# Two layers of FNet mixing and a spatial-shift MLP: normed rows kept on chip, z3 blocks ahead of w3 weights, operand work dealt over w4 steps

## The chip, the cores and the metric

The kernel runs on one core of a Trainium2 chip. The engines of a core run their own instruction lists side by side: PE (TensorE, the matrix engine), DVE (VectorE), ACT (ScalarE), POOL (GpSimd) and SP (SyncE), which here issues all transfers, one after the other in the order of the program. The metric is the device time of one execution in microseconds (us).

## The reference

The input x has 2048 rows (tokens) of 512 values. A layer adds a Fourier mixing and a shift MLP, and the whole is run twice with the same weights:

```python
def _A_ref(x, Cr, Ci, Dr, Di):              # FNet mixing
    a = x @ Dr.T ; b = x @ Di.T
    return Cr @ a - Ci @ b

def _B_ref(x, w1, w2, w3, w4):              # spatial-shift token mixing, channel MLP
    h  = gelu(layernorm(x) @ w1)
    g  = h with its four column quarters shifted by +1, -1, +2, -2 rows (zeros come in)
    x1 = x + g @ w2
    return x1 + gelu(layernorm(x1) @ w3) @ w4

for layer in range(2):
    x = x + _A_ref(layernorm(x), ...)
    x = x + _B_ref(layernorm(x), ...)
```

Cr and Ci are 2048 x 2048, Dr and Di 512 x 512, w1 and w2 512 x 512, w3 512 x 1376, w4 1376 x 512, all fp32.

## The kernel before

**Numbers.** Every fp32 operand is used as two fp32r parts: a high part, cast by ScalarE, and a low part, which VectorE makes as the operand minus its high part. A product takes three matmuls, high x high, high x low and low x high (`mm3`, L275 to L278).

**Fourier mixing.** The DFT matrices come in pieces of 512 KB from `in_ws` and `in_hs` into four buffers `raw`. `stage_one` (L207) makes the high part, or a difference and its high part, in one of four slots `ring`; `stage_two` (L233) makes the low part. `issue_dma` (L194) loads the next piece when a buffer is free, up to `state["load"]`; `state["limit"]` says up to which item operands are made ahead. The other operand is the normed rows. For each of the eight tiles of two row blocks, `xs[k]`, there are statistics (`xp_stats`), normed rows (`xp_norm`), sums and differences of their halves (`ax_sums`, `ay_sums`), their high parts and their low parts (`ax_highs`, `ay_highs`, `ax_lows`, `ay_lows`). The table `BACK` (L38) says after which step of a later phase rows of x1 are read back into `xs`.

**Shift MLP.** `by_pairs` (L753) treats the rows in four chunks of 512. For each chunk `shifted` does the w1 product and the gelu into `rg` (L653 to L659) and `mixed` the w2 product. Tables of functions, filled by `D(slot)` for VectorE and `A(slot)` for ScalarE (L900 to L990), say which operand work is done beside which step. `u_stats`, `finish` and `turn3` norm a chunk's rows and turn them; the turned rows z3 go to HBM (`z3d`) and are read back as blocks `b11f`, `b21f`, `b12f`, `b22f` (`b_in`, L738).

The w3 and w4 products are made for two pairs of chunks, one after the other. In a pair, five steps p make the w3 products of two blocks of the hidden width f each by seven products b1, b6, b5, b2, b7, b4, b3 of half blocks and of their sums, `bt1` to `bt4` (instead of eight), whose operands are parts of the w3 weights and of the z3 blocks. The results pass through the gelu into `hc` and are split into `h`. One chunk's w4 product follows in the steps beside them, and after the last p come the rest of its steps and thirteen steps of the other chunk, of 12 matmuls each (`w4_part`, L1003). Each w4 step uses one load of 512 KB (`w4_load`, L842); there are six slots, four in layer 0's second pair. `drain` (L1011) adds the accumulators to `xs` when a chunk's w4 product is done, and frees their banks.

In layer 0 the weights w3 and w4 are split once and written to HBM (`w3d`, `w4d`), and afterwards only read; `w3b` has two buffers of 1792 KB.

**What sets the order around the change.** All orders are written by hand, in program order. The list `bg` is emptied one function at a time by `one()` (L1021) in the p steps; `early` joins it in the last pair of layer 0, and `then[k]` (L1044) holds what `after_part(k)` (L1165) does behind w4 step k. These two lists make the next layer's first rows while this layer ends.

Of the kernel before, what the change touches and what calls it, by code (L numbers as in the profile page):

```python
# [8 lines left out]
F32 = mybir.dt.float32  # L9
# [28 lines left out]
BACK = {1: (0,), 2: (2,), 4: (4,)}  # L38
# [4 lines left out]
def spectral_mlp_kernel(ctx: ExitStack, tc: tile.TileContext, x, ws, hs, w1, w2, w34, out):  # L43
# [351 lines left out]


    mr_of = {}

    def ax_norm(k):
        mr_of[k] = xp[k]  # L400
        xp_norm(k)
# [351 lines left out]
    def by_pairs(layer, zs, xin, dst):  # L753
# [222 lines left out]
        if layer == 0:  # L976
# [8 lines left out]
            A(30, lambda: w4_high(0), lambda: w4_high(1))  # L985
            D(31, lambda: w4_low(0))
# [39 lines left out]
        early, then = [], [[] for _ in range(NF + 2)]  # L1026
        if not last_of(layer):

            def more():
                state.update(limit=w_items[1], load=len(pieces))  # L1030
                issue_dma()

            def do(f, k):
                return lambda: f(k)

            for k in range(4):
                early += [do(f, k) for f in (xp_stats, ax_norm, ax_sums, ax_highs, ax_lows)]
            early += [do(f, k) for f in (ay_back, ay_norm) for k in (0, 1)]
            for i, f, k in (
                *((0, ay_sums, 0), (0, ay_highs, 0), (0, ay_sums, 1), (0, ay_highs, 1)),  # L1040
                *((1, ay_lows, 0), (1, ay_back, 2), (2, ay_lows, 1), (2, ay_back, 3)),
                *((3, xp_stats, 4), (3, ay_norm, 2), (4, ay_sums, 2), (4, ay_highs, 2)),
                *((5, ay_lows, 2), (5, ay_norm, 3), (6, ay_sums, 3), (6, ay_highs, 3), (6, xp_norm, 4)),
                *((7, ay_lows, 3), (7, ax_sums, 4), (7, ax_highs, 4), (8, ay_sums, 4), (8, ax_lows, 4)),  # L1044
                *((8, ay_highs, 4), (9, xp_stats, 5), (10, ay_lows, 4), (10, xp_norm, 5)),
                *((11, ax_sums, 5), (11, ax_highs, 5), (12, ax_lows, 5)),
            ):
                then[i].append(do(f, k))
            then[1].insert(0, more)
            for i in (9, 11, 12):  # L1050
                then[i].append(lambda: ahead(1))

        for pair in range(n_pairs):
            c1, c2 = 2 * pair, 2 * pair + 1
            kept, next_too = layer or pair, pair == n_pairs - 1 and not last_of(layer)
            hcs = [hc[:, f] for f in range(NF)]
            if next_too:
                hcs[8:] = [hx[:, 0], hx[:, 1], rest[0]]
                bg += early
            bk, acc1 = (acc4, mm4) if pair == 0 else (mm4, acc4)  # L1060
            acc2 = [bk[(1 + i) % 4] for i in range(4)]
            if pair == 0:
                bg += [] if layer else [u_stats(2, 2)]
                bg += [finish(2, 0), finish(2, 2), turn3(turned, 2, 0, 1), turn3(turned, 2, 2, 3)]
                bg += [lambda: turn_out(turned, z3d[2])]
                z3_last = lambda t: [
                    *(u_stats(3, 0), u_stats(3, 2), finish(3, 0), finish(3, 2)),
                    *(turn3(t, 3, 0, 1), lambda: (turn3(t, 3, 2, 3)(), turn_out(t, z3d[3]))),
                ]
                bg += z3_last(turned if layer else tmp[:, 0:4])  # L1070
# [16 lines left out]
            def split_later(k):  # L1087
                if k < NF:
                    split(h4[(2 + k) % 4], hcs[fs[k]], act)

# [16 lines left out]
            for p in range(NF // 2):  # L1107
# [15 lines left out]
                add(u, u, b2)  # L1123
                low1 = gelu_high(h4[2 * (p % 2)], u)
# [7 lines left out]
                low1()  # L1132
                at_point(3)
# [17 lines left out]
                if kept or p + 2 >= NF // 2:  # L1151
                    w3_load(NF // 2 * pair + p + 2)
                one()

            if pair == 0:
                for c, names in ((2, ("11", "21")), (3, ("12", "22"))):
                    for half, to in enumerate(names):
                        b_in(c, half, to)
                bg += [sum_of("t1", "12", "11"), sum_of("t2", "22", "t1"), sum_of("t3", "22", "12"), sum_of("t4", "21", "t2")]
                bg += [parts(b) for b in ("11", "21", "12", "22", "t2", "t1", "t3", "t4")]  # L1160
# [4 lines left out]
            def after_part(k):  # L1165
                if next_too:
                    for f in then[k]:
                        f()
# [6 lines left out]
            for j in range(c1 * TC, c1 * TC + TC, 2):  # L1175
# [230 lines left out]
```

## Time and profile before

| | before |
|---|---|
| median of 3 runs (lowest to highest) | 1478.5 us (1477.55 to 1480.68) |
| profiled execution, its own time | 1479.15 us |
| its span in the trace | 1477.2 us |
| mean granted clock of TensorE | 0.994 |
| PE busy | 1452.9 us (98%), 6344 matmuls |
| DVE / ACT / POOL busy | 1121.6 / 721.9 / 80.5 us |
| moved by transfers | 288.97 MB, 196 GB/s mean |

Busy times are those of one profiled execution; its span is 1.95 us shorter than its time, which also holds what lies around the first and the last instruction. Times of events below are counted from the start of the span. A matmul counts as busy while it waits in the pipeline, so a busy share of 98% does not by itself say that TensorE ran at its pace; the count of matmuls in a window of 20 us says it.

### The profile page before, as it was taken

The page shows a single profiled execution, that of the slowest core. Times are in us where ns is not written, and L with a number is a line of the kernel's source. Part 1 is how long each engine was busy: PE and PEld are TensorE (multiplying, and loading weights), DVE is VectorE, ACT ScalarE, POOL GpSimd, SP SyncE. Part 2 cuts the span into 40 slices and gives each one's busy share as a digit, 9 for nine tenths or more (in the row PEclk, how much of TensorE's full clock was granted, in tenths as well). Part 3 has the DMA queues.
Part 4 walks back from the last instruction along what each step waited for, and adds up shares of the span by engine and source line. Part 5 has one row for each costly group of instructions (what it writes and reads, how often), then busy time and mean ns, then how long its engine had stood idle before and what let it go on. Part 6 is the DMA issues. An engine that isn't in the chain of part 4 may idle for free.

```text
span 1477.2 us, 17273 instructions
## 1 busy us (share of the span) xinstructions
PE 1452.9 (98%) x6344; PEld 1189.0 (80%) x6344; DVE 1121.6 (76%) x1553; ACT 721.9 (49%) x966; POOL 80.5 (5%) x111
## 2 busy tenths in 40 slices
PE   9999999999999999899889999999999999999998
PEld 7888888888878787688767888888888788888887
DVE  6876987988868897566589879979888688646443
ACT  5563454444567655344545544544445675333231
POOL 2100000000001000000010000000000010000000
PEclk9999999999999999999999999999999999999999
DMA  6326556566546678845635465565565457758434
GB/s 238 133 87 212 191 189 212 179 199 236 179 136 178 214 254 280 327 151 185 243 113 173 169 199 200 185 202 194 185 236 184 141 165 274 224 213 300 158 131 157
DMA packets 111876, 288.97 MB, mean 196 GB/s; under 512 B 8496, under 2 KB 37168, under 8 KB 109232
## 3 DMA queue, kind: packets, MB, share of 16 engines
q1 hardware_dynamic: 111792, 287.87, 57.8%
q8 instruction: 50, 0.82, 0.2%
q14 instruction: 34, 0.28, 0.1%
HBM read 243.01 MB, written 44.83 MB: 195 GB/s over the span
## 4 chain that ended last, share of the span: by engine, by line
PE 83%; DVE 9%; DMA 4%; ACT 2%; issue 1%; POOL 1%; SPq 0%; DVEq 0%; ACTq 0%; POOLq 0%
PE psd L276 9%; PE psd L277 9%; PE psd L278 9%; PE psa L276 7%; PE psa L278 7%; PE psa L277 7%; PE psc L278 6%; PE psc L276 6%; PE psc L277 6%; PE psb L278 6%; PE psb L276 6%; PE psb L277 6%; DMA w4r<-w4d 2%; DVE ring L239 2%; DMA raw<-in_ws 1%
## 5 line engine op out<-in xcount | busy, mean ns | idle before, releaser
L223 ACT CAST ring<-raw 128x1024 fp32r<-128x1024 f32 x127 | 132.8, 1054 | 100.1 <-PE psd L278 48.9
L239 DVE TENSOR_TENSOR ring<-raw,ring 128x1024 fp32r<-128x1024 f32 x127 | 154.6, 1221 | 26.8 <-ACT ring L223 26.8
L276 PE MATMUL psd<-ring,rr 128*128 128x512 f32 x208 | 80.9, 389 | 0.0
L277 PE MATMUL psd<-ring,rr 128*128 128x512 f32 x208 | 80.9, 389 | 0.0
L278 PE MATMUL psd<-ring,rr 128*128 128x512 f32 x208 | 80.9, 389 | 0.0
L653 ACT ACTIVATE tmp<-rest 128x512 f32<-128x512 f32 x32 | 20.3, 633 | 82.4 <-DVE rest L473 82.1
L316 POOL TENSOR_TENSOR rs<-ve,mhalf 128x4 f32<-128x4 f32 x16 | 26.8, 1678 | 612.8 <-DVE nm L315 612.8
L656 DVE TENSOR_TENSOR h<-hc,h 128x512 fp32r<-128x512 f32 x41 | 27.9, 689 | 38.3 <-ACT h L659 38.2
L659 ACT CAST h<-hc 128x512 fp32r<-128x512 f32 x41 | 25.5, 621 | 64.4 <-PE psc L277 26.9
L230 ACT CAST ring<-ring0f 128x1024 fp32r<-128x1024 f32 x28 | 29.6, 1056 | 54.3 <-DVE ring0f L229 54.3
L324 ACT ACTIVATE tmp<-xs,nb,rs 128x512 f32<-128x512 f32 x58 | 44.8, 810 | 23.1 <-POOL nb L296 23.1
L239 DVE TENSOR_TENSOR ring<-ring1f,ring 128x512 fp32r<-128x512 f32 (+1 forms) x56 | 53.3, 952 | 0.8 <-ACT ring L226 0.8
L295 POOL TENSOR_TENSOR rs<-ve,mhalf 128x2 f32<-128x2 f32 (+1 forms) x33 | 30.2, 914 | 429.8 <-DVE nb L294 429.8
L276 PE MATMUL psc<-ring,ay 128*128 128x512 f32 x128 | 49.9, 390 | 0.3 <-ACT rr11f L498 0.3
L277 PE MATMUL psc<-ring,ay 128*128 128x512 f32 x128 | 50.0, 391 | 0.2 <-DVE ring L239 0.2
L278 PE MATMUL psc<-ring,ay 128*128 128x512 f32 x128 | 49.8, 389 | 0.0
L276 PE MATMUL psb<-ring,ay 128*128 128x512 f32 x128 | 49.8, 389 | 0.0
L277 PE MATMUL psb<-ring,ay 128*128 128x512 f32 x128 | 49.8, 389 | 0.0
L278 PE MATMUL psb<-ring,ay 128*128 128x512 f32 x128 | 49.8, 389 | 0.0
L276 PE MATMUL psd<-ring,ay 128*128 128x512 f32 x126 | 49.0, 389 | 0.0
L276 PE MATMUL psa<-ring,ay 128*128 128x512 f32 x126 | 49.0, 389 | 0.0
L277 PE MATMUL psd<-ring,ay 128*128 128x512 f32 x126 | 49.0, 389 | 0.0
(450 smaller groups left out, 4451.6 us busy)
## 6 DMA issues: line engine op xcount, KB each, us to landing
raw<-in_ws SPq DMA_DIRECT2D x183, 512.0 KB, 4.9
w4r<-w4d SPq DMA_DIRECT2D x77, 512.0 KB, 3.7
raw<-in_hs SPq DMA_DIRECT2D x56, 512.0 KB, 3.5
w3b<-w3d SPq DMA_DIRECT2D x15, 1792.0 KB, 7.3
w3d<-w3b SPq DMA_DIRECT2D x5, 1792.0 KB, 6.7
x1d<-tmp SPq DMA_DIRECT2D x12, 512.0 KB, 6.3
xs<-x1d SPq DMA_DIRECT2D x12, 512.0 KB, 6.7
w4d<-w4r SPq DMA_DIRECT2D x11, 512.0 KB, 7.4
```

The source lines that it names most:

```text
L223: nc.scalar.copy(dest[:, a:b, 0], r[0][:, a:b])
L230: nc.scalar.copy(dest[:, :, 0], lo)
L239: nc.vector.tensor_tensor(lo, src, hi.bitcast(F32), op=ALU.subtract)
L276: nc.tensor.matmul(o, lh, rh, start=first, stop=False)
L277: nc.tensor.matmul(o, lh, rl, start=False, stop=False)
L278: nc.tensor.matmul(o, ll, rh, start=False, stop=last)
L295: nc.gpsimd.tensor_tensor(rs[:, :n], ve[:, :n], mhalf[:, 0, :n], op=ALU.pow)
L316: nc.gpsimd.tensor_tensor(rs, ve, mhalf[:, :, :2], op=ALU.pow)
L324: nc.scalar.activation(o, s, AF.Identity, bias=mr[2], scale=mr[1])
L653: nc.scalar.activation(g_of, ps_of, AF.Gelu_apprx_tanh)
L656: nc.vector.tensor_tensor(dst[:, 1], g, dst[:, 0].bitcast(F32), op=ALU.subtract)
L659: copy(dst[:, 0], g)
```

## The change

- `norm_in_place` norms tiles 2 and 3 of the next layer's rows into `xs` itself, so that the sums made later read them there. Before, such tiles were written to `x2d` and read back through `tmp` (`ay_back`) and normed again (`ay_norm`).
- The reads of the second pair's z3 blocks are placed in the last p step of the first pair, ahead of further w4 loads; the two w3 loads move behind them into the w4 steps.
- The raw loads, row writes, sums and parts between and after the pairs are dealt over the w4 steps by `then` for both pairs; before, raw loads were issued in one go and the row work lay in other steps.
- In the table beside `shifted`, the parts of the blocks and of their sums are in another order, and the parts of t3 and t4 move into the pair loop. `u_stats(3, 2)` moves behind `finish(2, 2)`.
- At the start, the low part of item 1 is made in two halves, the first tile is normed in halves, up to four items are made ahead instead of two, and the low parts of tile 1 come ahead of a low part of the ring.
- One read back of x1 rows moves from step 4 to step 6.

The core of the diff:

```diff
-BACK = {1: (0,), 2: (2,), 4: (4,)}
+BACK = {1: (0,), 2: (2,), 6: (4,)}
...
-        nc.vector.tensor_tensor(lo, src, hi.bitcast(F32), op=ALU.subtract)
+        for i in ((1, 0) if n == 1 else (slice(0, b - a),)):
+            nc.vector.tensor_tensor(lo[:, i], src[:, i], hi[:, i].bitcast(F32), op=ALU.subtract)
...
-    def ay_back(k):
-        xp[k] = pairs[k % 2]
-        rows(xp[k], x2d, 2 * k, 2, True)
-
-    def ay_norm(k):
+    def norm_in_place(k):
         for i in range(2):
-            normed_act(xp[k][:, i], xp[k][:, i], mr_of[k][i])
+            normed_act(xs[k][:, i], xs[k][:, i], xp[k][i])
+        xp[k] = xs[k]
...
-        A(26, highs("12"))
-        D(27, sum_of("t2", "22", "t1"), sum_of("t4", "t4", "t2"))
-        A(27, highs("22"))
-        D(28, lows("12", "22"))
-        A(28, highs("t2", "t1"))
-        D(29, lows("t2", "t1"))
+        A(27, highs("12", "22"))
+        D(28, sum_of("t2", "22", "t1"), sum_of("t4", "t4", "t2"))
+        A(28, highs("t1", "t2"))
+        D(29, lows("12", "22"))
         A(29, highs("t3", "t4"))
-        D(30, lows("t3"))
-        D(31, lows("t4"))
+        D(31, lows("t2", "t1"))
...
-            early += [do(f, k) for f in (ay_back, ay_norm) for k in (0, 1)]
-            for i, f, k in (
-                *((0, ay_sums, 0), (0, ay_highs, 0), (0, ay_sums, 1), (0, ay_highs, 1)),
-                *((1, ay_lows, 0), (1, ay_back, 2), (2, ay_lows, 1), (2, ay_back, 3)),
...
-            then[1].insert(0, more)
+        def more(n):
+            state.update(limit=w_items[1], load=min(w_pieces[0] + n, len(pieces)))
+            issue_dma()
...
+            early += [do((f, k)) for f in (xp_stats, norm_in_place if k > 1 else xp_norm, ax_sums, ax_highs, ax_lows)]
...
+            steps = (
+                ((ay_lows, 2), (ay_sums, 3), (ay_highs, 3), (more, 1)),
+                ((ay_lows, 3),),
+                ((xp_stats, 4), (keep_rows, 8)),
+                ((xp_norm, 4), (xp_stats, 5), (more, 2)),
+                ((xp_sums, 4), (xp_highs, 4), (xp_norm, 5)),
+                ((ax_lows, 4), (more, 3)),
+                ((ay_lows, 4), (ax_sums, 5), (ax_highs, 5)),
+                ((ax_lows, 5), (more, 4)),
+                ((ahead, 1), (keep_rows, 10)),
+                ((ahead, 1), (more, len(pieces))),
+                ((ahead, 1),),
+                (),
+                (),
+            )
...
-                bg += [finish(2, 0), finish(2, 2), turn3(turned, 2, 0, 1), turn3(turned, 2, 2, 3)]
...
+                bg += [lows("t3", "t4")]
                 bg += [] if layer else [u_stats(2, 2)]
+                bg += [u_stats(3, 0), finish(2, 0), finish(2, 2), u_stats(3, 2)]
+                bg += [turn3(turned, 2, 0, 1), turn3(turned, 2, 2, 3), lambda: turn_out(turned, z3d[2])]
+                bg += [finish(3, 0), finish(3, 2), turn3(t, 3, 0, 1)]
...
+                if pair == 0 and p == NF // 2 - 1:
+                    next_blocks((3, 0, "12"), (2, 0, "11"))
...
+                    next_blocks((2, 1, "21"))
...
-                if kept or p + 2 >= NF // 2:
+                if kept and not (pair == 0 and p >= NF // 2 - 2):
                     w3_load(NF // 2 * pair + p + 2)
...
+                next_blocks((3, 1, "22"))
+                then[1] = [lambda: w3_load(NF // 2)]
+                then[2] = [lambda: rows(xs[0], dst, 0, 2, False)]
...
-                normed(pairs[0][:, 0], xt(0), xp[0][0])
+                norm_half(0, 1)
+                norm_half(0, 0)
                 part_highs(0)
+                block_low(1)
                 xp[0] += stats([xt(1)])
-                block_low(1)
...
-                state["limit"] = 2
+                state["limit"] = 4
...
+                        if not k:
+                            xp_main_lows(1)
                     else:
-                        if k + 1 < NP:
+                        if 0 < k < NP - 1:
                             xp_main_lows(k + 1)
```

TensorE's and POOL's instructions stand in the same order in both programs; the order moves on SP, VectorE and ScalarE. Three places are shown here, first before, then in the changed kernel. Names end in a number for the tile, `w4d1` is the part of the split w4 weights for f = 1, `x <- y` is a write of x from y.

SP at the end of layer 0's first pair, before: the turned rows of chunk 3 are written, then the weights of the w4 steps and of the next pair and the next pair's z3 blocks are read.

```order
L622 DMA z3d3_83<-tmp_68 32x16x128 x4
L869 DMA w3b1_198<-w3d0_84 128x3584
L850 DMA w4r2_211<-w4d1_91 128x1024
L859 DMA w4d8_98<-w4r4_215 128x1024
L859 DMA w4d9_99<-w4r5_217 128x1024
L850 DMA w4r3_213<-w4d2_92 128x1024
L869 DMA w3b0_196<-w3d1_85 128x3584
L739 DMA b11f_181<-z3d2_82 128x2x512
L739 DMA b21f_183<-z3d2_82 128x2x512
L739 DMA b12f_185<-z3d3_83 128x2x512
L739 DMA b22f_187<-z3d3_83 128x2x512
L850 DMA w4r4_215<-w4d3_93 128x1024
```

The same place in the changed kernel:

```order
L612 DMA z3d3_83<-tmp_68 32x16x128 x4
L729 DMA b12f_185<-z3d3_83 128x2x512
L729 DMA b11f_181<-z3d2_82 128x2x512
L729 DMA b21f_183<-z3d2_82 128x2x512
L840 DMA w4r2_211<-w4d1_91 128x1024
L849 DMA w4d8_98<-w4r4_215 128x1024
L849 DMA w4d9_99<-w4r5_217 128x1024
L840 DMA w4r3_213<-w4d2_92 128x1024
L729 DMA b22f_187<-z3d3_83 128x2x512
L840 DMA w4r4_215<-w4d3_93 128x1024
L840 DMA w4r5_217<-w4d4_94 128x1024
L859 DMA w3b1_198<-w3d0_84 128x3584
```

The z3 blocks moved ahead of four w4 loads and of two writes, and the two w3 loads to the rear of them.

SP in the w4 steps of layer 0's second pair, before: `raw` are pieces of the DFT matrix for layer 1, `x2d` the rows on their way to layer 1.

```order
L850 DMA w4r3_213<-w4d2_92 128x1024
L205 DMA raw0_176<-in_ws 128x1024
L205 DMA raw1_177<-in_ws 128x1024
L205 DMA raw2_178<-in_ws 128x1024
L205 DMA raw3_179<-in_ws 128x1024
L196 DMA tmp_68<-x2d_79 128x2x512
L196 DMA x2d_79<-xs4_146 128x2x512
L196 DMA x2d_79<-xs5_147 128x2x512
L850 DMA w4r0_207<-w4d3_93 128x1024
L196 DMA tmp_68<-x2d_79 128x2x512
L850 DMA w4r1_209<-w4d4_94 128x1024
```

The same stretch in the changed kernel:

```order
L840 DMA w4r2_211<-w4d1_91 128x1024
L205 DMA raw0_176<-in_ws 128x1024
L840 DMA w4r3_213<-w4d2_92 128x1024
L840 DMA w4r0_207<-w4d3_93 128x1024
L196 DMA x2d_79<-xs4_146 128x2x512
L840 DMA w4r1_209<-w4d4_94 128x1024
L205 DMA raw1_177<-in_ws 128x1024
L840 DMA w4r2_211<-w4d5_95 128x1024
L840 DMA w4r3_213<-w4d6_96 128x1024
L205 DMA raw2_178<-in_ws 128x1024
L840 DMA w4r0_207<-w4d7_97 128x1024
```

The four raw loads are now dealt among the w4 loads, and the reads of x2d into `tmp` are gone.

VectorE just ahead of the last drain of layer 0 (the rows that write `xs6` and `xs7`), before: the lows of rows 4 and 5 and the first items of the ring.

```order
L389 TENSOR_TENSOR ay4_109<-tmp_68,ay4_109 128x2x256
L355 TENSOR_TENSOR ax5f_128<-tmp_68 128x2x256
L356 TENSOR_TENSOR ax5f_128<-tmp_68 128x256
L225 TENSOR_TENSOR ring1f_171<-raw0_176 128x512
L239 TENSOR_TENSOR ring1_170<-ring1f_171,ring1_170 128x512
L381 TENSOR_TENSOR ax5_127<-ax5f_128,ax5_127 128x3x256
L239 TENSOR_TENSOR ring2_172<-raw1_177,ring2_172 128x2x512
L1013 TENSOR_TENSOR xs6_148<-psd1_243,xs6_148 128x512
L1013 TENSOR_TENSOR xs6_148<-psa0_236,xs6_148 128x512
L1013 TENSOR_TENSOR xs7_149<-psa1_237,xs7_149 128x512
L1013 TENSOR_TENSOR xs7_149<-psd0_242,xs7_149 128x512
```

The same place in the changed kernel:

```order
L382 TENSOR_TENSOR ax5_127<-ax5f_128,ax5_127 128x3x256
L646 TENSOR_TENSOR h43_203<-hx_206,h43_203 128x512
L240 TENSOR_TENSOR ring0_168<-raw0_176,ring0_168 128x2x512
L646 TENSOR_TENSOR h40_200<-hx_206,h40_200 128x512
L225 TENSOR_TENSOR ring1f_171<-raw0_176 128x512
L240 TENSOR_TENSOR ring1_170<-ring1f_171,ring1_170 128x512
L240 TENSOR_TENSOR ring2_172<-raw1_177,ring2_172 128x2x512
L1001 TENSOR_TENSOR xs6_148<-psd1_243,xs6_148 128x512
L1001 TENSOR_TENSOR xs6_148<-psa0_236,xs6_148 128x512
L1001 TENSOR_TENSOR xs7_149<-psa1_237,xs7_149 128x512
L1001 TENSOR_TENSOR xs7_149<-psd0_242,xs7_149 128x512
```

The lows and sums of rows 4 and 5 stand ahead of the last splits of h (`h40` to `h43`); behind those only the ring's lows and one difference are left ahead of the drain.

## Rows read from the trace of the kernel before

**Rows 1.** the page's busy times of the engines, share of the span, instructions

```profile
PE 1452.9 (98%) x6344; PEld 1189.0 (80%) x6344; DVE 1121.6 (76%) x1553; ACT 721.9 (49%) x966; POOL 80.5 (5%) x111
```

**Rows 2.** TensorE's waits: line that waited <- what ended it: us in all, times, longest

```profile
PE psa L276 <- DVE xs L1013: 4.6, 1, 4.6
PE psc L276 <- DMA w4r<-w4d: 4.4, 1, 4.4
PE psd L276 <- DMA w4r<-w4d: 4.4, 1, 4.4
...
PE psa L278 <- DVE rg L656: 1.3, 2, 0.6
PE psb L278 <- DVE rr L351: 1.2, 1, 1.2
PE psb L276 <- ACT rest L1113: 1.2, 1, 1.2
PE psc L277 <- DVE ring L239: 0.7, 2, 0.5
PE psa L276 <- ACT rg L659: 0.4, 1, 0.4
...
PE psc L278 <- DVE rr L434: 0.2, 1, 0.2
```

**Rows 3.** windows: busy us (instructions) by engine, granted clock, DMA share, GB/s

```profile
480.00:500.00 20.00, 18.32 (x77) 14.00 (x76) 19.32 (x30) 12.62 (x19) 1.69 (x2) 1.00 0.73 234
600.00:620.00 20.00, 15.56 (x57) 12.16 (x56) 12.01 (x13) 6.07 (x9) 0.00 (x0) 0.83 0.87 339
720.00:740.00 20.00, 15.61 (x62) 12.28 (x61) 7.42 (x15) 8.99 (x14) 0.89 (x2) 0.91 0.90 328
740.00:760.00 20.00, 15.45 (x65) 12.27 (x64) 14.97 (x27) 7.90 (x11) 2.36 (x2) 0.93 0.20 68
760.00:780.00 20.00, 19.50 (x78) 15.56 (x78) 18.67 (x35) 13.85 (x20) 3.22 (x4) 0.90 0.45 149
1160.00:1180.00 20.00, 20.00 (x88) 16.16 (x87) 12.64 (x22) 11.47 (x16) 1.09 (x3) 1.00 0.54 173
```

**Rows 4.** the chain that ended last, its two waits for weights: start, us, what

```profile
594.97 13.35 DMA w4r<-w4d
...
718.74 11.39 DMA w4r<-w4d
```

**Rows 5.** SP's timeline, 572 to 610: start us, us, engine, line, transfer, count

```profile
573.96 6.05 SPq L622 DMA_DIRECT2D z3d<-tmp  x4
...
584.41 1.40 SPq L859 DMA_DIRECT2D w4d<-w4r  x2
```

**Rows 6.** DMA issues by kind, 575 to 625: count, KB each, median us to landing

```profile
z3d<-tmp SPq DMA_DIRECT2D x4, 256.0 KB, 7.6
...
w4d<-w4r SPq DMA_DIRECT2D x2, 512.0 KB, 10.7
```

**Rows 7.** the page's DMA issues over the whole span, columns as in group 6

```profile
w4r<-w4d SPq DMA_DIRECT2D x77, 512.0 KB, 3.7
```

**Rows 8.** SP's timeline, 713 to 731

```profile
715.07 1.91 SPq L205 DMA_DIRECT2D raw<-in_ws  x4
```

**Rows 9.** TensorE's timeline, 749 to 766

```profile
753.79 0.39 PE L278 MATMUL psb<-ring,ax 128*128 128x512 f32 x1
```

**Rows 10.** VectorE's timeline, 743 to 776

```profile
757.30 0.69 DVE L1013 TENSOR_TENSOR xs<-psd,xs 128x512 f32<-128x512 f32 x1
...
774.51 1.22 DVE L239 TENSOR_TENSOR ring<-raw,ring 128x1024 fp32r<-128x1024 f32 x1
```

**Rows 11.** VectorE's timeline, 494 to 508

```profile
497.86 0.68 DVE L656 TENSOR_TENSOR rg<-extra,rg 128x512 fp32r<-128x512 f32 x1
```

**Rows 12.** ScalarE's timeline, 553 to 563

```profile
560.23 1.52 ACT L324 ACTIVATE rest<-rest,nb,rs 128x512 f32<-128x512 f32 x2 [0.89 <-DVE xs L718]
```

**Rows 13.** VectorE's timeline, 3 to 21

```profile
17.43 2.36 DVE L239 TENSOR_TENSOR ring<-raw,ring 128x1024 fp32r<-128x1024 f32 x2 [4.55 <-ACT ring L223]
```

More of the change, by code (lines that the diff above doesn't have):

```diff
@@ L984, in by_pairs @@
             A(28, lambda: w3_keep(0))
-            A(30, lambda: w4_high(0), lambda: w4_high(1))
-            D(31, lambda: w4_low(0))
+            A(29, lambda: w4_high(0))
+            D(30, lambda: w4_low(0))
+            A(30, lambda: w4_high(1))
         else:
@@ new lines, in do, with keep_rows @@
+        def do(*fks):
+            return lambda: [f(k) for f, k in fks]
+        def more(n):
+            state.update(limit=w_items[1], load=min(w_pieces[0] + n, len(pieces)))
+            issue_dma()
+        def keep_rows(j):
+            rows(xs[j // 2], dst, j, 2, False)
+        early = []
+        for k in range(4):
+            early += [do((f, k)) for f in (xp_stats, norm_in_place if k > 1 else xp_norm, ax_sums, ax_highs, ax_lows)]
+        early += [
+            do((ay_sums, 1), (ay_highs, 1)),
+            do((ay_sums, 0), (ay_highs, 0)),
+            do((ay_lows, 1)),
+            do((ay_lows, 0)),
+            do((ay_sums, 2), (ay_highs, 2)),
+        ]
@@ new lines, in next_steps @@
+        def next_steps():
+            steps = (
[13 more added lines that the diff above has]
+            )
+            return [[do(*s)] for s in steps]
@@ L1053, in by_pairs @@
         for pair in range(n_pairs):
             c1, c2 = 2 * pair, 2 * pair + 1
-            kept, next_too = layer or pair, pair == n_pairs - 1 and not last_of(layer)
+            kept, next_too = bool(layer or pair), pair == n_pairs - 1 and not last_of(layer)
             hcs = [hc[:, f] for f in range(NF)]
@@ L1059, in by_pairs @@
                 bg += early
+            if pair:
+                bg.insert(0, lows("t4"))
             bk, acc1 = (acc4, mm4) if pair == 0 else (mm4, acc4)
@@ L1089, in split_later, with next_blocks @@
                     split(h4[(2 + k) % 4], hcs[fs[k]], act)
+            def next_blocks(*which):
+                for c, half, to in which:
+                    b_in(c, half, to)
             def w_prep(p):
@@ L1132, in by_pairs @@
                 low1()
+                if pair == 0 and p == NF // 2 - 1:
+                    next_blocks((2, 1, "21"))
                 at_point(3)
@@ L1150, in by_pairs @@
                 gelu(hcs[2 * p], x)
-                if kept or p + 2 >= NF // 2:
+                if kept and not (pair == 0 and p >= NF // 2 - 2):
                     w3_load(NF // 2 * pair + p + 2)
                 one()
+            then = [[] for _ in range(NF + 2)]
             if pair == 0:
[L1156 to L1160, printed above, removed]
+                next_blocks((3, 1, "22"))
+                then[1] = [lambda: w3_load(NF // 2)]
+                then[2] = [lambda: rows(xs[0], dst, 0, 2, False)]
+                then[3] = [lambda: rows(xs[1], dst, 2, 2, False)]
+                then[4] = [sum_of("t1", "12", "11"), sum_of("t2", "22", "t1")]
+                then[5] = [sum_of("t3", "22", "12"), sum_of("t4", "21", "t2"), highs("11", "21")]
+                names = "11", "21", "12", "22", "t2", "t1", "t3", "t4"
+                for i in range(6):
+                    then[6 + i] = [lows(names[i]), highs(names[i + 2])]
+                then[8] += [lambda: w3_load(NF // 2 + 1)]
+                then[12] = [lows("t3")]
+            if next_too:
+                then = next_steps()
             if next_too:
@@ L1165, in after_part @@
             def after_part(k):
-                if next_too:
-                    for f in then[k]:
-                        f()
+                for f in then[k]:
+                    f()
             for i in range(2):
@@ L1174, in by_pairs @@
             drain(c1, acc1)
-            for j in range(c1 * TC, c1 * TC + TC, 2):
-                rows(xs[j // 2], dst, j, 2, False)
+            if pair and not next_too:
+                for j in range(c1 * TC, c1 * TC + TC, 2):
+                    rows(xs[j // 2], dst, j, 2, False)
             split_later(2)
@@ L1230, in block_low, with norm_half @@
                     )
+                def norm_half(i, h):
+                    v = slice(h * DH, (h + 1) * DH)
+                    normed(pairs[0][:, i, v], xt(i)[:, v], xp[0][i])
                 halves = [pairs[0][:, i].rearrange("p (h d) -> p h d", h=2) for i in range(2)]
```

30 lines of the change are left out of this document (2 added, 28 removed).

## The prediction

> **What bounds the kernel now.** I read the page's busy times first: TensorE is busy 1452.9 us, 98% of the span [rows 1], so a change that leaves its 6344 matmuls alone can win only what TensorE waits or runs below its pace. The matmuls stand in the same order in both programs, so the question is which waits go. The list of TensorE's waits gives them [rows 2]: three of 4.4 to 4.6 us stand out (one for the vector engine's `xs` at L1013, two for `w4r<-w4d` loads), and the rest are of 0.2 to 1.3 us.
>
> A wait is not all that a place costs. The windows show it [rows 3]: a full 20 us of this stage holds 88 matmuls at clock 1.00, so one takes 20/88 = 0.227 us. 600 to 620 holds 57, 31 too few, or 7.0 us: 4.4 of wait and 2.6 in which the matmuls behind it ran at a lower granted clock (0.83 is a mean of the two levels, 1.2 and 2.4 GHz). 720 to 740 holds 62, 26 too few, 5.9 us. 740 to 760 and 760 to 780 hold 65 and 78, 33 too few, 7.5 us. Those three places are 20.4 us of 1479.15. The window 480 to 500, with three short waits, still shows clock 1.00.
>
> **The change part by part.**
>
> *z3 blocks ahead of the weights (7.0 us at 603.6).* The chain of waits says that the load which TensorE waited for was issued at 594.97 and took 13.35 us to land, at 608.32 [rows 4]. It was issued late because its slot is freed by a write `w4d<-w4r`, issued 584.41 [rows 5], which takes 10.7 us here [rows 6]: 584.41 + 10.7 = 595.1. It landed late because two `w3b` loads of 1792 KB and the four z3 blocks of 512 KB were in flight. TensorE wanted it at 608.32 - 4.4 = 603.9. In the changed SP order the block `b12f` stands right behind the four z3d3 writes, two more blocks after it, then `w4r2`, the two `w4d` writes, `w4r3`, `b22f`, and then this load; both `w3b` loads come after. The first block must wait for the writes: SP issued them from 573.96 to 580.01 [rows 5], 7.6 us to landing [rows 6], so by 587.6 at the latest, and all SP work behind it waits too. From there to the end of the wanted load nine transfers of 512 KB (0.524 MB each) must pass, 4.72 MB; at the 339 GB/s of 600 to 620 [rows 3] that is 13.9 us, so 601.5: 2.4 us ahead of need. By latency instead: the writes issued about 588.6, 10.7 to landing, 599.3; then the load, between 3.7 us (median of all such loads) [rows 7] and the 13.35 that it took among the `w3b` loads, so 603.0 to 612.7. The lower end saves everything, the upper one costs some 4 us more than now. I take the bytes, since just the 3.67 MB of `w3b` that made the 13.35 leave the stretch: **-7.0**. The `w4r2` load now goes out some 588.9 instead of 583.7, but with four transfers ahead lands by 594; twelve matmuls use one load (2.7 us), so it is wanted at 603.9 - 5.5 = 598.4. The two `w3b` loads are wanted only by the next pair.
>
> *Raw loads and row writes dealt over w4 steps (5.9 us at 725.5).* The load for which TensorE waited went out at 718.74 and took 11.39 us, to 730.13 [rows 4]. Ahead of it SP had issued four raw loads at 715.07 [rows 8], a `tmp<-x2d` read and two `x2d` writes. In the changed order one raw load stands there, between two w4 loads. Six transfers less are 3.1 MB; at the 328 GB/s of 720 to 740 [rows 3] 9.6 us. So it lands not before 718.74 + 3.7 = 722.4 [rows 7] and not after about 724, wanted at 730.13 - 4.4 = 725.7. The four re-reads of x2d are gone altogether, because the normed rows stay in `xs`. A w4 load per 2.7 us is 190 GB/s and the dealt loads add one for every two or three: under what the queue moved. **-5.9**; if one dealt load still collides, half.
>
> *Row work two steps earlier (5.8 us at 753.8).* TensorE did its twelve matmuls of the next phase up to 753.79 [rows 9] and then had to wait until the accumulators were drained. Vector started the drain at 757.30 [rows 10], because the sums, stats and lows of rows 4 and 5 stood ahead of it. Accumulation had ended twelve matmuls before 753.79 + 0.23, at 751.3, so the drain can begin about 751.5 if vector is free; in the changed order the row work of tiles 4 and 5 sits up to ten instructions earlier, between lows of h. Behind the last low of h there are then only three instructions of the ring ahead of the drain, which wait for nothing late. Behind the drain the next 24 vector rows are the same as before, up to the low that ends at 774.51 + 1.22 [rows 10] and that TensorE waited for again (0.7 us in two [rows 2]). That chain is nearly gapless, so it becomes the limit: all of it moves by 757.30 - 751.5 = 5.8 us, and not by more, to end at 769.9; TensorE without its wait and slow stretch would be there at 775.7 - 7.5 = 768.2 or a little before. **-5.8** of the 7.5 lost there; a rest of 1 to 2 us shows up as a wait at the ring low, at about 769. Bounds: 2.9 (the drain gets only half as early, another row instruction late) to 7.5.
>
> *Shifted stage, rg high and low earlier.* TensorE waited 1.3 us in two for the vector's rg low and 0.4 for the cast [rows 2]. The second low started at 497.86 behind two 1.22 us sums [rows 11] that now follow it, and its cast now precedes the 1.05 us cast of b12. The first 0.6 stays (its low stands where it stood). So 1.1 goes, with the lengthened matmuls behind each wait 1.3: **-1.3** (0.8 to 1.6). The lows of t3 and t4 (2 x 1.22 us) move into the pair loop.
>
> *Pair loop, stats moved.* The 1.2 us wait for the copy L1113 [rows 2] came from two norm activations of 1.52 us at 560.23 ahead of the copy [rows 12]; u_stats(3, 2) now stands a step later, so it goes. But p = 0 now has the t3 and t4 lows and u_stats(3, 0) besides, and those norms stand before the next copy: a like wait of 0.7 is easy to make there. **-0.6** (0 to -1.3, or +0.3 if both meet).
>
> *First tiles.* The 1.2 us for `rr` L351 [rows 2] came behind two ring lows of 2.36 us together [rows 13]; now rr and ay stand ahead of ring3's low, ring2's and ring3's casts come before the norms, and the two normed halves go in reverse. One 1.22 low less ahead of it, and the cast before it: **-1.4** (0.6 to 1.8).
>
> *x1d read four transfers later.* **-0.2**: the wait for rr L434 [rows 2]; its bound above is 0.4, below zero.
>
> Sum: 7.0 + 5.9 + 5.8 + 1.3 + 0.6 + 1.4 + 0.2 = 22.2 us, so 1479.15 - 22.2 = 1457.0 for a profiled execution. That one was 0.65 us over the median of 1478.5, so I forecast **1456.3 us**. None of the added instructions (two halves for one low, norms in place) is on TensorE. Layer 1 has the same code at its pairs and its window there is full (88 in 1160 to 1180 [rows 3]), so it has nothing to win and only the rivals below can cost there.
>
> **The rivals.**
>
> *A: the z3 block's wait keeps the weights late.* If the load takes 9 us or more behind the writes, as the upper end of the latency sum has it, it lands no earlier than now, at 608, and the 7.0 us stay: 1463.3. For it: SP is one queue, and `w4r2` and the writes wait behind `b12f`. Against: the bytes.
>
> *B: vector becomes the limit from the drain on.* With the drain only half as early that part gives 2.9: 1459.2. For it: vector is the busiest engine from 740 to 780, 18.67 us of 20 in the second half [rows 3].
>
> *C: short waits of TensorE hold the clock down.* If the 1 to 2 us that remain at 769 cost what the 4.4 us wait cost behind it (2.6 us), the time is 1458.9. Against: 480 to 500 has three short waits and clock 1.00 [rows 3]. The Trainium skill, TensorE: Matmul & The Clock Gate, section A second HAM failure mode: psum-queue depth-cycling, describes a kernel whose frequent micro-idles between matmul groups made the clock oscillate and degraded throughput by the cost between bursts; by it the waits dealt out in this stage would cost more than their length. The trace does not agree so far: 1.00 there.
>
> *D: everything goes.* No rest at 769, no new wait in the pair loop: 7.0 + 5.9 + 7.5 + 1.6 + 1.3 + 1.8 + 0.4 = 25.5 us off 1478.5, which gives 1453.0.
>
> *E: the waits come back elsewhere.* The two waits for weights are replaced by waits of the same length for the blocks and the raw pieces, and the drain's by one for the ring: 1478, no change.
>
> *F: slower.* SP stands at `b12f` in both layers, in layer 1 where nothing waits now. Each microsecond that the z3d3 writes land past the margin is a microsecond of TensorE, and the first 2.6 more of low clock. Without the 7.0 the other parts win 15.2; to reach 3 us over, the layers must lose 18.2: (d - 4.4) + (d + 2.6) = 18.2, d = 10 us past need in each. That is 7.6 us to landing grown to about 20. Against: the writes are x4 of 256 KB and with `w3b` gone fewer transfers compete. If it happens, 1482 or more.
>
> **How the numbers follow.** Chances: forecast 0.68 (own range 1453.5 to 1459), A 0.13, B 0.05, C 0.04, D 0.04, E 0.02, F 0.04. 0.2%, or 3 us, is about what a measurement of this kernel can tell from no change. Faster is all but E and F, 0.94; same 0.02; slower 0.04. The range goes from D less 2 us for the lengthened matmuls around the small waits, which the sum leaves out, 1451, to A with its pair-loop wait worse by 1.5, 1465.
>
> **What would show it.** In the changed profile: no wait for `w4r<-w4d` over 1 us, and 88 matmuls in each 20 us of both pairs' w4 steps; the drain's first vector instruction within 1 us of the last w4 matmul, and a wait for a ring low of 1 to 2 us some 15 us on; the clock at 1.00 there; and no wait for rr L351 over 0.3 us. Wrong would be: `b12f` issued later than 588 less the 4 us that are won before it, the wanted w4 load issued after 597, TensorE waiting in layer 1's w4 steps, or the copy in p = 0 or 1 waiting more than 1 us.

## The result and the profile after

The changed kernel takes 1454.99 us (median of 4, 1454.74 to 1456.22) against 1478.4 (median of 4, 1477.55 to 1480.68). The ratio is 0.9841, 95% interval 0.9824 to 0.9858: faster, by 1.6%. The profiled execution took 1455.18 us, with a span of 1453.0 us, 24.2 shorter than before. The forecast was 1456.3, so the size was right within 1.3 us; below it turns out that one of its terms rests on a wrong cause and that misses of several terms cancel.

The page's busy times, as in [rows 1]:

```profile
PE 1444.6 (99%) x6344; PEld 1184.2 (82%) x6344; DVE 1121.2 (77%) x1555; ACT 715.8 (49%) x958; POOL 80.6 (6%) x111
```

TensorE's waits, as in [rows 2]:

```profile
PE psc L277 <- ACT rest L1120: 1.5, 1, 1.5
...
PE psc L277 <- ACT rr11f L488: 0.3, 1, 0.3
PE psa L279 <- DVE rg L646: 0.3, 1, 0.3
PE psd L277 <- ACT h L649: 0.3, 1, 0.3
PE psc L278 <- DVE ring L240: 0.2, 1, 0.2
```

The three waits of 4.4 to 4.6 us are gone, and so are those for `rr`, for the rg cast and for the x1 rows. One of more than 0.3 us is new: 1.5 us for the copy `rest` (L1120, L1113 before); it stands at another place than the old one. The lines left out are two waits that lie in the first 10 us.

Windows of TensorE's stretch, columns as in [rows 3]:

```profile
480.00:500.00 20.00, 19.67 (x86) 15.74 (x85) 17.44 (x27) 13.42 (x19) 1.69 (x2) 1.00 0.73 261
520.00:540.00 20.00, 18.47 (x81) 14.84 (x80) 17.86 (x37) 10.74 (x18) 2.23 (x4) 1.00 0.74 275
580.00:600.00 20.00, 20.00 (x89) 16.26 (x88) 12.62 (x17) 6.57 (x10) 0.00 (x0) 1.00 0.92 342
600.00:620.00 20.00, 20.00 (x88) 16.27 (x87) 14.00 (x16) 9.04 (x11) 0.00 (x0) 1.00 0.99 401
700.00:720.00 20.00, 20.00 (x87) 15.80 (x85) 13.10 (x28) 9.47 (x16) 2.16 (x4) 1.00 0.81 284
720.00:740.00 20.00, 19.68 (x83) 15.31 (x83) 16.50 (x25) 8.60 (x13) 0.00 (x0) 1.00 0.65 213
740.00:760.00 20.00, 19.75 (x87) 16.04 (x86) 19.36 (x35) 13.73 (x20) 3.21 (x4) 1.00 0.34 109
```

Where 57, 62 and 65 matmuls stood, there are now 83 to 89, and the clock is 1.00 throughout. 720 to 740 is still 5 short.

The matmuls are the same 6344 in the same order, so the start of the n-th can be compared between the two traces. The difference grows by what a place gained (pair 0 and pair 1 are layer 0's first and second pair of chunks; the parts are rounded):

| place (time in the trace before) | forecast | gained |
|---|---|---|
| first tiles, to 21 | 1.4 | 2.0 |
| x1 rows read, 380 to 391 | 0.2 | 0.6 |
| shifted stage, 415 to 508 | 1.3 | 2.3 |
| pair loop, 530 and 562 | 0.6 | -0.8 (-1.8 and +1.0) |
| w4 steps of pair 0, 608 to 614 | 7.0 | 7.2 |
| w4 steps of pair 1, 730 to 743 | 5.9 | 4.9 (6.0, then 1.1 given back) |
| drain and what follows, 758 to 776 | 5.8 | 7.5 |
| sum, with 0.2 later | 22.2 | 24.0 |

SP at the end of pair 0, as in [rows 5], and the transfer of the load issued at 591.17, as in [rows 6]:

```profile
572.53 5.09 SPq L612 DMA_DIRECT2D z3d<-tmp  x4
581.22 0.38 SPq L729 DMA_DIRECT2D b12f<-z3d  x1
...
583.24 0.88 SPq L849 DMA_DIRECT2D w4d<-w4r  x2
...
591.17 1.76 SPq L840 DMA_DIRECT2D w4r<-w4d  x2
592.99 0.42 SPq L859 DMA_DIRECT2D w3b<-w3d  x1
```

```profile
w4r<-w4d SPq DMA_DIRECT2D x1, 512.0 KB, 5.2
```

The block goes out at 581.22 after the z3d3 writes, the two `w4d` writes at 583.24, and the load that TensorE once waited for at 591.17. It lands at 591.2 + 5.2 = 596.4. TensorE starts the first matmul of its step without a break:

```profile
599.47 0.39 PE L279 MATMUL psc<-w4r,h 128*128 128x512 f32 x1
599.70 0.39 PE L277 MATMUL psc<-w4r,h 128*128 128x512 f32 x1
```

So the load is there 3.3 us ahead of need; the working with bytes had 2.4. The `w3b` load follows at 592.99.

The drain, on VectorE as in [rows 10] and on TensorE as in [rows 9]:

```profile
733.51 0.68 DVE L1001 TENSOR_TENSOR xs<-psd,xs 128x512 f32<-128x512 f32 x1
...
750.72 1.22 DVE L240 TENSOR_TENSOR ring<-raw,ring 128x1024 fp32r<-128x1024 f32 x1
```

```profile
734.05 0.39 PE L279 MATMUL psa<-w4r,h 128*128 128x512 f32 x1
...
734.74 0.40 PE L279 MATMUL psd<-w4r,h 128*128 128x512 f32 x1
...
737.53 0.39 PE L279 MATMUL psb<-ring,ax 128*128 128x512 f32 x1
737.75 0.39 PE L277 MATMUL psa<-ring,ax 128*128 128x512 f32 x1
```

Vector begins to drain at 733.51, before the last w4 matmul at 734.74, and the matmul that waited 4.6 us now starts at 737.75, 0.22 behind the one before it. The whole vector chain behind it came forward by 757.30 - 733.51 = 23.79 us, of which 16.26 had been won before this place (the matmul ahead of the wait starts at 737.53 instead of 753.79), so 7.5 here.

### The profile page after: what moved, and what is told of

It is laid out like the page before. It is cut to its first block, busy times and chain, and to the rows that moved or that the text cites. A ratio compares the mean times of both kernels' runs of the same rounds, so it can differ in the third digit from the quotient of the medians.

```text
span 1453.0 us, 17281 instructions
## 1 busy us (share of the span) xinstructions
PE 1444.6 (99%) x6344; PEld 1184.2 (82%) x6344; DVE 1121.2 (77%) x1555; ACT 715.8 (49%) x958; POOL 80.6 (6%) x111
## 4 chain that ended last, share of the span: by engine, by line
PE 89%; DVE 6%; ACT 2%; DMA 1%; issue 1%; POOL 0%; SPq 0%; DVEq 0%; ACTq 0%; POOLq 0%
PE psd L277 9%; PE psd L279 9%; PE psd L278 9%; PE psa L277 7%; PE psa L279 7%; PE psa L278 7%; PE psc L277 7%; PE psc L279 7%; PE psc L278 7%; PE psb L277 6%; PE psb L279 6%; PE psb L278 6%; DVE ring L240 1%; DMA zt1f<-zd 1%; DVE st L291 0%
## 5 line engine op out<-in xcount | busy, mean ns | idle before, releaser
L240 DVE TENSOR_TENSOR ring<-raw,ring 128x1024 fp32r<-128x1024 f32 (+1 forms) x128 | 154.7, 1212 | 23.0 <-ACT ring L223 23.0
L277 PE MATMUL psa<-ring,ay 128*128 128x512 f32 x126 | 49.0, 389 | 0.0
L278 PE MATMUL psa<-ring,ay 128*128 128x512 f32 x126 | 49.0, 389 | 0.0
```

Source lines behind the costliest of these rows:

```text
L240: nc.vector.tensor_tensor(lo[:, i], src[:, i], hi[:, i].bitcast(F32), op=ALU.subtract)
L277: nc.tensor.matmul(o, lh, rh, start=first, stop=False)
L278: nc.tensor.matmul(o, lh, rl, start=False, stop=False)
```

## The experiments

Times without a range are of one run; beside them stand 1454.99 for the changed kernel and, on the same chips, 1477.5 to 1479.1 for the one before. What a part does at its own place is read from the starts of the same matmuls.

**What made the weights late in pair 0: the w3 loads or the blocks' place?** Two halves of that part are undone one at a time.

In d_w3_first:

```diff
-                if kept and not (pair == 0 and p >= NF // 2 - 2):
+                if kept or p + 2 >= NF // 2:
...
-                then[1] = [lambda: w3_load(NF // 2)]
...
-                then[8] += [lambda: w3_load(NF // 2 + 1)]
```

In d_z3_late:

```diff
-                if pair == 0 and p == NF // 2 - 1:
-                    next_blocks((3, 0, "12"), (2, 0, "11"))
...
-                if pair == 0 and p == NF // 2 - 1:
-                    next_blocks((2, 1, "21"))
...
-                next_blocks((3, 1, "22"))
+                next_blocks((2, 0, "11"), (2, 1, "21"), (3, 0, "12"), (3, 1, "22"))
```

> The changed kernel with its z3 blocks where the change put them, but the two w3 loads of 1792 KB back in the last two steps p, ahead of the w4 loads. Theory (bytes): the 3.67 MB of w3 are what made the wanted w4 load late, so TensorE waits for it again, 3 to 6 us and the slow stretch behind it, 5 to 8 us more than the changed kernel's 1455. Rival (the blocks' place is what matters): the blocks are early here, so no wait, within 0.5 us of the changed kernel.

Measured 1464.6 us, 9.6 more. SP, TensorE's wait and the windows in d_w3_first:

```profile
585.72 0.38 SPq L729 DMA_DIRECT2D b12f<-z3d  x1
...
589.30 0.44 SPq L859 DMA_DIRECT2D w3b<-w3d  x1
...
596.97 1.94 SPq L840 DMA_DIRECT2D w4r<-w4d  x3
```

```profile
PE psc L277 <- DMA w4r<-w4d: 6.3, 3, 3.9
```

```profile
580.00:600.00 20.00, 17.55 (x76) 13.79 (x75) 9.20 (x13) 6.34 (x10) 0.00 (x0) 1.00 0.88 308
600.00:620.00 20.00, 16.11 (x59) 12.66 (x58) 11.35 (x13) 8.28 (x12) 0.00 (x0) 0.83 0.82 316
```

With the two w3 loads ahead the three loads behind them are late one after the other, 6.3 us in three waits, and the matmuls behind the longest (3.9) run at a lower clock (0.83 in the window). It is more than expected: a w3 load now stands ahead of the z3d3 writes and these land late too, so the block goes out at 585.72 instead of 581.22, the `w4d` writes wait behind it, and the freed slot's load goes out at 596.97 instead of 591.17.

> The changed kernel with the w3 loads in the w4 steps, where the change put them, but the four z3 blocks back behind the last p step, in the old order. Theory (bytes): the same bytes pass ahead of the wanted load, only in another order, so no wait for w4 weights over 0.5 us and the time within 1 us of 1455. Rival (the blocks' place is what matters): the wait for the load comes back, 4 to 7 us more.

Measured 1455.13 us, and the end of the last matmul is within 0.01 us of the changed kernel's. The blocks' place is worth nothing here. The part that works is the w3 loads' later place.

On the kernel before, b_w3_late:

```diff
-                if kept or p + 2 >= NF // 2:
+                if kept and not (pair == 0 and p >= NF // 2 - 2):
...
+                if pair == 0 and k in (1, 8):
+                    w3_load(NF // 2 + k // 8)
```

> The kernel before with one part of the change only: the two w3 loads of layer 0's and layer 1's first pair go out behind w4 steps 1 and 8 instead of in the last two steps p; the z3 blocks stay where they were. Theory (the 3.67 MB of w3 alone made the load late): no wait for that load, 7.1 us gained at 608 and kept, 1471. Rival (the blocks ahead are needed too in the old order): under 3 us gained.

Measured 1472.46 us. The wait falls from 4.4 to 0.4 us, and the gain by 614 is 7.97 - 0.76 = 7.2 us; the 0.4 left, for a later load, takes 0.6 of it back. Over the whole program it is 6.5: other places differ by up to 1.7 either way.

**What made the load late in pair 1: raw loads or the x2d transfers?**

In e_raw_once:

```diff
-                ((ay_lows, 2), (ay_sums, 3), (ay_highs, 3), (more, 1)),
+                ((ay_lows, 2), (ay_sums, 3), (ay_highs, 3), (more, len(pieces))),
```

On the kernel before, b_raw_dealt:

```diff
-            then[1].insert(0, more)
+            for i, n in ((1, 1), (4, 2), (6, 3), (8, 4), (9, len(pieces))):
+                then[i].insert(0, do(more, n))
```

> The changed kernel, but the raw loads after the first w4 step of layer 0's second pair may all go out at once (four, as many as there are buffers), with the reads of x2d still gone. Theory (bytes, 0.52 MB each at about 0.4 MB/us): three more transfers ahead make the next w4 load land 3.8 us later; its landing was 3.7 us and it has about 8.4 us from issue to need, so the wait is under 0.5 us and the old wait of 4.4 us needed the x2d transfers as well. Rival (the raw loads alone made it): a wait of 3 us or more, 3 to 6 us more in all.

Measured 1454.84 us, no wait for weights. The load behind the four raw loads lands later, but in time:

```profile
w4r<-w4d SPq DMA_DIRECT2D x1, 512.0 KB, 8.0
```

That is 8.0 us of the 8.4 that the expectation gave it, where the changed kernel's took 3.7. The dealing of the raw loads is not needed once the x2d reads are gone, but little was left.

> The kernel before with one part of the change only: its raw loads behind the w4 steps of layer 0's second pair dealt out (one at step 1, one more at 4, 6 and 8, all at 9), the x2d reads still there. Theory (bytes, either part is enough): three transfers of 0.52 MB less ahead of the wanted load bring it 3.8 us earlier, so the wait of 4.4 us falls under 1 us, without the slow stretch: 4.5 to 6 us less than before's 1478. Rival (the x2d transfers alone made the wait, as all raw loads at once cost nothing without them): the wait stays above 3 us, under 1.5 us gained.

Measured 1475.86 us. TensorE's waits in b_raw_dealt:

```profile
PE psa L276 <- DVE xs L1013: 6.1, 1, 6.1
...
PE psd L276 <- DMA w4r<-w4d: 0.7, 1, 0.7
```

The wait for weights falls from 4.4 to 0.7 and 5.0 us are won there, as expected; but the next one, for the drain, grows from 4.6 to 6.1. The whole is only some 3 us faster. So either part alone nearly removes the load's wait, and the drain's wait takes back a part: vector's drain did not come forward as far as TensorE did.

**What made the drain late?** The forecast blamed the row work of tiles 4 and 5; ring items, too, stand ahead of the drain. Four other lists for the changed kernel:

In f_rows_late, and then the lines of the list that differ in f_rows_before:

```diff
-            return [[do(*s)] for s in steps]
+            return [[]] * 2 + [[do(*s)] for s in steps[:-2]]
```

```diff
...
+                ((keep_rows, 8),),
+                ((xp_stats, 4), (more, 2)),
...
+                ((more, 3),),
+                ((xp_norm, 4),),
+                ((ax_sums, 4), (ax_highs, 4), (more, 4)),
+                ((ay_sums, 4), (ax_lows, 4), (ay_highs, 4), (ahead, 1), (keep_rows, 10)),
+                ((xp_stats, 5), (ahead, 1), (more, len(pieces))),
+                ((ay_lows, 4), (xp_norm, 5), (ahead, 1)),
+                ((ax_sums, 5), (ax_highs, 5)),
+                ((ax_lows, 5),),
```

In f_ring_late; f_both joins it with f_rows_before:

```diff
-                ((ahead, 1), (keep_rows, 10)),
+                ((keep_rows, 10),),
                 ((ahead, 1), (more, len(pieces))),
-                ((ahead, 1),),
-                (),
                 (),
+                ((ahead, 1),),
+                ((ahead, 1),),
```

> The changed kernel with the whole list of next-layer work behind the w4 steps of layer 0's second pair moved two steps later. Theory (the drain waits on vector behind the row work of tiles 4 and 5): the drain's first instruction starts 4 to 6 us later against TensorE's last w4 matmul, and all of that is paid, with the slow clock behind it: 4 to 8 us more. Rival (only the start of the chain, not its place, matters; a chain is long anyhow): under 1 us more.

> The changed kernel with the row work of tiles 4 and 5 at the steps that it had before (stats of 5 behind step 9 instead of 3, its norm at 10 instead of 4, its sums at 11 instead of 6, its lows at 12 instead of 7), the ring items and raw loads as changed. Theory: vector reaches the drain late because of the chain stats, POOL, norm, sums of tile 5, so the wait ahead of the drain comes back, 3 to 7 us more than 1455. Rival (the ring items' place ahead of the drain made it): under 1.5 us more, as with the list moved by two steps, which cost 1.1.

> The changed kernel with only the three ring items behind the w4 steps at their steps of before (9, 11, 12 instead of 8, 9, 10). Theory (rows of tile 5): vector is free there, so under 1 us more. Rival (ring items): the last item's cast and low stand right ahead of the drain, 3 us or more.

> The changed kernel with both the row work of tiles 4 and 5 and the three ring items at their steps of before. Theory (each is harmless or nearly so alone: 2.4 and -0.4 us; together the ring items stand behind the late rows in vector's and ScalarE's order): the drain starts 6 to 7.5 us after it could and the wait ahead of it is above 3 us with the slow clock behind it, 5 to 8 us more than 1455. Rival (some other part of the change, such as the x2d reads gone, freed the drain): 2 to 3 us more, as with the rows alone.

Measured 1456.26, 1457.34, 1454.75 and 1457.21 us. My theory fell. With the row work of tiles 4 and 5 and the ring items all at their old steps (f_both) the drain begins 2 us later than in the changed kernel, and only that is lost, at the ring low behind it; TensorE's waits and the drain's start in f_both:

```profile
PE psc L278 <- DVE ring L240: 2.5, 2, 1.6
...
PE psa L277 <- DVE xs L1001: 0.2, 1, 0.2
```

```profile
735.56 0.68 DVE L1001 TENSOR_TENSOR xs<-psd,xs 128x512 f32<-128x512 f32 x1
```

The cause was further back, on ScalarE. Its timeline in the kernel before:

```profile
726.30 1.52 ACT L324 ACTIVATE tmp<-tmp,nb,rs 128x512 f32<-128x512 f32 x2 [8.40 <-DMA tmp<-x2d]
...
731.52 1.52 ACT L324 ACTIVATE tmp<-tmp,nb,rs 128x512 f32<-128x512 f32 x2
```

A norm (L324) stood 8.40 us for the read of x2d into `tmp`, the second one followed at 731.52, when its read, issued at 720.61 and 10.9 us in flight, had landed. ScalarE's casts of h, and vector's lows and row work, stand in order behind them. From the second norm to the drain are 757.30 - 731.52 = 25.78 us. In b_raw_dealt, where fewer transfers were in the way:

```profile
722.47 1.52 ACT L324 ACTIVATE tmp<-tmp,nb,rs 128x512 f32<-128x512 f32 x2 [4.86 <-DMA tmp<-x2d]
...
727.85 1.52 ACT L324 ACTIVATE tmp<-tmp,nb,rs 128x512 f32<-128x512 f32 x2 [0.20 <-DMA tmp<-x2d]
```

```profile
753.62 0.68 DVE L1013 TENSOR_TENSOR xs<-psd,xs 128x512 f32<-128x512 f32 x1
```

Here 753.62 - 727.85 = 25.77 us: the same chain, hung on the landing of the second read. In b_w3_late the second norm, the drain and one POOL instruction between them (it belongs to the statistics of tile 5; the last line is the same instruction in the kernel before) are:

```profile
723.96 1.52 ACT L324 ACTIVATE tmp<-tmp,nb,rs 128x512 f32<-128x512 f32 x2
```

```profile
749.17 0.68 DVE L1013 TENSOR_TENSOR xs<-psd,xs 128x512 f32<-128x512 f32 x1
```

```profile
742.32 0.19 POOL L296 TENSOR_TENSOR nb<-nb,rs 128x2 f32<-128x2 f32 x1
```

```profile
749.90 0.75 POOL L296 TENSOR_TENSOR nb<-nb,rs 128x2 f32<-128x2 f32 x1
```

The chain is 749.17 - 723.96 = 25.21 us there, shorter by what that instruction took less. In f_both, which has no such reads, late rows and ring items cost 2.1. So some 2 us of the 7.5 come from the new steps and, as an estimate, some 5 from the reads that are gone: without its 4.86 us of idle ScalarE, b_raw_dealt's wait of 6.1 would be 1.2. Two things stay open. That the reads alone would do it was not tried in a kernel of its own. And f_both has the norms of tiles 2 and 3 at their early place, as the changed kernel does, while in the kernel before they stand in these w4 steps behind the reads: what the reads cost and what this work cost there was not told apart. The chain of the same length behind the read in three kernels and the small loss without the reads carry the rest.

**The small parts and the new wait.**

In s_small_back the table `BACK`, the halves, `norm_half`, `state["limit"]`, `xp_main_lows` and the D and A tables beside the shifted stage are as before, and:

```diff
-                bg += [lows("t3", "t4")]
+                bg += [lambda: None]
```

> The changed kernel with three small parts undone: the first tiles, the step of the x1 read back, and the order of parts and sums beside the shifted stage (with an empty function in the place of the lows of t3 and t4 in the background list). By the places where the changed kernel gained: 1.9 us at 20, 0.6 at 380 to 391, 2.3 at 495 to 508 come back as losses, 4.8 us, and the wait of 1.5 us for the copy at 527 stays, since the norms keep their slot: 1459.8. Rival for that copy (it is the lows of t3 and t4 that fill vector): the wait goes, 1458.

Measured 1458.42 us: 2.3 come back at 20, some 1.4 at 493 to 503, nothing at 380 to 391. The read's place did nothing; that stretch differs by up to 0.6 between two kernels that are alike there (the one before and b_w3_late). The copy's wait falls from 1.5 to 0.7, between both theories: the lows of t3 and t4 make about half of it. ScalarE in the changed kernel shows the other half:

```profile
525.54 1.52 ACT L325 ACTIVATE tmp<-tmp,nb,rs 128x512 f32<-128x512 f32 x2 [0.89 <-DVE xs L708]
526.97 0.56 ACT L1120 COPY rest<-psc 128x512 f32<-128x512 f32 x1
```

Two norms wait for vector until 525.54 and the copy stands behind them. Moving the norms from the end of a step p to a place behind a w4 step:

In layer 0 of c_finish_mid:

```diff
-                bg += [u_stats(3, 0), finish(2, 0), finish(2, 2), u_stats(3, 2)]
-                bg += [turn3(turned, 2, 0, 1), turn3(turned, 2, 2, 3), lambda: turn_out(turned, z3d[2])]
-                bg += [finish(3, 0), finish(3, 2), turn3(t, 3, 0, 1)]
+                bg += [finish(2, 0), u_stats(3, 0), finish(2, 2), u_stats(3, 2)]
+                bg += [turn3(turned, 2, 0, 1), turn3(turned, 2, 2, 3), finish(3, 0)]
+                bg += [lambda: turn_out(turned, z3d[2]), finish(3, 2), turn3(t, 3, 0, 1)]
```

> The changed kernel with, in layer 0's first pair, two functions of the background list exchanged twice, so that the norms of finish(2, 0) and finish(3, 0) come behind a w4 step instead of at the end of a step p, ahead of the next step's copy. Theory (TensorE waits for the copy because those norms stand ahead of it): the waits of 1.5 and 0.1 us for the copy go with the lengthened matmuls behind them, 2.0 us less: 1453. Rival (vector is full there with the lows of t3 and t4, so another wait takes its place): 1454.5 to 1455.5.

Measured 1453.27 us (4 runs, 1453.2 to 1454.27), all below the changed kernel's lowest; the trace gives 1.8 us. That much is won at the copy; a small new wait, 0.2 us for `rest` (L463) at 538, takes its place in part, and some 0.4 are won elsewhere.

**A version that beats both.** The 1.1 us given back at 720 to 727 has the same form: ScalarE's casts of h behind two norms, in the changed kernel:

```profile
718.32 1.52 ACT L325 ACTIVATE tmp<-xs,nb,rs 128x512 f32<-128x512 f32 x2
719.74 1.12 ACT L649 CAST h<-hc 128x512 fp32r<-128x512 f32 x2
```

The version best has the lines of c_finish_mid, and:

```diff
-                ((xp_sums, 4), (xp_highs, 4), (xp_norm, 5)),
-                ((ax_lows, 4), (more, 3)),
-                ((ay_lows, 4), (ax_sums, 5), (ax_highs, 5)),
-                ((ax_lows, 5), (more, 4)),
-                ((ahead, 1), (keep_rows, 10)),
+                ((xp_sums, 4), (xp_highs, 4)),
+                ((ax_lows, 4), (xp_norm, 5), (more, 3)),
+                ((ay_lows, 4),),
+                ((ax_sums, 5), (ax_highs, 5), (more, 4)),
+                ((ax_lows, 5), (ahead, 1), (keep_rows, 10)),
```

> The changed kernel with the two exchanges of the background list and, besides, tile 5's norm, sums and lows one w4 step later, so that ScalarE's casts of h don't stand behind its norms. Theory: 1.8 us from the exchanges, and of the 1.0 us lost at 720 to 727 most comes back, less up to 0.5 at the ring low of 752: 1452.7 (1452.2 to 1453.3). Rival (the later rows delay the drain's chain as much as they free the casts): 1453.3 to 1454.3.

Measured 1452.24 us (5 runs, 1452.13 to 1452.77), ratio to before 0.9819 (0.9806 to 0.9833). All five runs lie below all of the changed kernel's and of c_finish_mid's. Its waits from 500 to 760, one late and one new, and the window that was 5 short:

```profile
PE psc L278 <- DVE ring L240: 0.4, 1, 0.4
...
PE psb L277 <- DVE rest L463: 0.2, 1, 0.2
```

```profile
720.00:740.00 20.00, 20.00 (x88) 16.27 (x87) 16.87 (x25) 8.30 (x13) 0.00 (x0) 1.00 0.61 209
```

## Why the prediction was right, and where its steps failed

- *Weights of pair 0, 7.0:* right in size (7.2) and in cause, the w3 loads; bytes were the right choice over latencies. That the z3 blocks' place matters is in the heading of that part and not in its sum; d_z3_late shows it doesn't. Rival A, where the block's wait keeps the weights late, did not happen.
- *Weights of pair 1, 5.9:* 6.0 at the place. The prediction took all six transfers together; e_raw_once and b_raw_dealt show that dropping either group nearly does. The 1.1 given back (norms ahead of casts of h) was not foreseen.
- *Drain, 5.8:* the sum was low by 1.7 and the step failed in its cause. "Vector started the drain at 757.30 [rows 10], because the sums, stats and lows of rows 4 and 5 stood ahead of it" took what stood next in order for the reason; those had been late themselves, for a read of x2d on ScalarE's queue. The size came out near because the change removes the reads too: that is luck. Where it was mis-sized: "the drain can begin about 751.5" counted from the end of all accumulation, but banks are drained one by one, and the first is done nine matmuls before the last. Vector began 1.2 us before the last w4 matmul, so of the "rest of 1 to 2 us" at the ring low only 0.2 remained, and the place gave the 7.5 that rival D had for it.
- *Pair loop, -0.6:* wrong sign, 0.8 us lost. The like wait that was called easy to make was made, 1.5 us and not 0.7, by the lows and by norms at the end of a step p.
- *First tiles 1.4, shifted stage 1.3:* 2.0 for the tiles (2.3 when undone), 2.3 for the stage (1.4 when undone). *x1 read, 0.2:* not shown; undoing it changes nothing.
- *Rival C, the clock:* 1.00 in every window with a wait of 0.2 to 1.5 us, 520 to 540 among them. The oscillation that the Trainium skill, TensorE: Matmul & The Clock Gate, section A second HAM failure mode: psum-queue depth-cycling, describes does not show here: the wait of 1.5 us left 81 matmuls of 88 in its window, 1.6 us. The wait of 3.9 us in d_w3_first lies in a window at 0.83, like those of 4.4 before (0.83 and 0.91).
- *Rival B and F:* vector was the limit of nothing long, and SP's stop at the block (577.62 to 581.22 at most) cost nothing in either layer.
- *The signs:* the block's issue (581.22), the wanted load's issue (591.17) and the clock came as forecast. Three did not: 720 to 740 holds 83 matmuls and not 88, the wait at the ring low was 0.2 us and not 1 to 2, and the copy waited 1.5 us, which stood among the signs of being wrong.
- *The sum:* that it was near, 22.2 against 24.0, is in part luck. The drain gave 1.7 more than forecast and the tiles and the shifted stage 1.6; the pair loop gave 1.4 less and pair 1 1.0 less.

## What to carry to other kernels

An engine that is late at a hand-over is to be followed back through its own order until it last stood idle for something outside: here from VectorE over ScalarE to a read of rows that could have stayed on chip. A load that arrives late is priced by the bytes in flight ahead of it; here moving the largest transfers, which nobody needed yet, was worth 7 us, and the order among the needed ones nothing. A gain at one wait may be handed to the next; the same matmul's start in both traces shows it place by place.

## What the runs showed of the hardware

The median 512 KB load of w4 weights took 3.7 us in the kernel before, and 11.4 and 13.35 us at the two places where TensorE waited for it, in windows that moved 328 and 339 GB/s. With three more raw loads of the same size ahead, the same load took 8.0 us (e_raw_once) instead of 3.7 (changed kernel), 1.4 us for each: its time in flight was mostly the queue ahead. And the wait for one read on ScalarE's in-order queue reached VectorE's drain 25.78, 25.77 and 25.21 us behind the norm that had waited, in three kernels; the shorter one had a POOL instruction on the way of 0.19 us instead of 0.75, so the way had next to no slack.
